# Where the weights of a feed-forward block lie between the forward and the backward pass of a decode step

## The chip, the core and the metric

The kernel runs on one core of a Trainium2 chip. The metric is device time in microseconds (us) of one execution, lower is better. The engines are TensorE (PE; its weight loads are PEld), VectorE (DVE), ScalarE (ACT), GpSimd (POOL) and SyncE (SP). Each works through its own queue in order. In this kernel SP issues the loads, POOL issues the stores, and 16 DMA engines carry both.

## What is computed

One token passes through a transformer block, and then the gradients of the block are formed. All tensors are bfloat16. Cut to what matters:

```python
h = layernorm(x) * (1 + ca) + sa            # sa, ca, ga, sb, cb, gb = silu(c) @ w_mod
q = (h @ wq)                                # 32 heads of 192
p = softmax(q @ k_cache.T * 192 ** -0.5)    # per head, 8192 keys
x1 = x + ga * ((p @ v_cache) @ wo)
h = layernorm(x1) * (1 + cb) + sb           # = xb
x2 = xb + hs(xb); x2 = x2 + gelu(layernorm(x2) @ w3) @ w4
out = x1 + gb * x2                          # D = 640, w3 640x1536, w4 1536x640
# and the gradients of x, k_cache, v_cache, wq, wo, w3, w4, c, w_mod for a given grad_out
```

(With a single token the shifted part `hs` is zero.) The outputs are `out` and the nine gradients. The K and V caches are 32 x 8192 x 192 each, 101 MB each, and their gradients are as large, so nearly all bytes are those four tensors.

## The kernel before, in words

**Tiles.** A head's K or V is handled in two half tiles of 128 partitions x 32 x 192 (1,536 KB, 1.57 MB). K has five buffers (`KB`, 0 to 4), V three (`VB`, 0 to 2). A further tile of this size has the tag `prod`: products of the scores in the forward pass, `pq` in the backward pass, and `w4a` in between. `w4b` (128 x 3840) holds pieces of w4, and `stg` of the same size is the staging tile of the backward. The backward pass also has `do_r`, `v_bc`, `dao_bc`, `wT` and two `er_b` tiles.

**Forward (lines 503 to 592).** A loop runs over heads 0 to 30. SP loads the next K and V halves as buffers come free (L344, L298), DVE and PE form the scores, ACT and DVE scale V by the softmax weights, PE accumulates K^T V for the later dq.

**Middle (L596 to L769, then L859 to L908).** Head 31 is done by itself: `score_mul` (L602) multiplies the K halves into `pb`, `score_tree` (L606) sums them on PE, `o_rows` (L407) forms the output. `pair_o` and `pair_ao` give x1. Then come two layernorms folded into one chain of small reductions (L709 to L741), u = w3^T n2 as 60 matmuls (L745), the gelu and its derivative on DVE and one exponential on ACT (L751 to L769), the product of du with the transposed w3 (60 matmuls, L875), a chain to `dao_bf` (L897), the products of wo with it (`do_mm`, L832), and the 60 matmuls of h2 = w4^T g (L857, `h2_mm`).

Where the weights lie in the middle:
- w3 rows 0 to 511 in `VB[0]` and the rest in a `vs` tile (L648, L650); w4 rows as `w4b` (blocks 0 to 3) and `w4a` (4 to 11, one load, L659); blocks 0 to 2 are loaded a second time into `stg` (L859).
- The transposed w3 goes to `VB[1]` (nine blocks) and `w4b` (three). `w3t` makes it in twelve groups of five PE transposes and one ACT copy (L667, L668), with a PSUM tile of two buffers. Five groups stand before the u matmuls, seven or eight behind.
- `dg_part` (L500) forms one entry of w4 dbo per block on DVE; twelve calls are strewn over the end of the forward pass and the middle.

**Backward (from L910).** 64 steps s go through the half heads, from head 31 down. In each step PE forms dV as outer products (`dv_groups`, L951; copied by ACT, L952), DVE forms V times do (`mul_q`, L931) and PE sums it (`tree_q`, L940) to dP, then DVE forms dK (`dk_part`, L956), and POOL stores both (L1193). The first five output tiles lie in `OB = (VB[1], KY, KE, VB[1], KD)`, where `KY`, `KE`, `KD` are K buffers. The first V tiles needed are those of head 31, still in `KY` and `VB[2]`; the third is loaded again into `VB[0]` (L918).

`late_rows` (L914) runs in the first step: dw4 is made row block by row block on DVE (L847), nine blocks in `VB[0]` and three in `stg`, and stored by POOL (L850). Other outputs and weights are side jobs: a list (L1135 on) from which `slot()` takes about one piece per call, four calls in each step. The order on each queue is the order of the code; the regions marked `manual_schedule` keep it, and small independent DVE operations may be moved between dependent ones.

Of the kernel before, what the change touches and what calls it, by code (L numbers as in the profile page):

```python
# [8 lines left out]
FP32 = mybir.dt.float32  # L9
# [11 lines left out]
def kernel(  # L21
# [27 lines left out]
    P = 128  # L49
# [277 lines left out]
    OB = (VB[1], KY, KE, VB[1], KD)  # L327
# [11 lines left out]
    with tc.tile_pool(name="vs", bufs=3) as vsp, tc.tile_pool(name="ft", bufs=2) as ft, \  # L339
            tc.tile_pool(name="psM", bufs=2, space=PS) as psM, tc.tile_pool(name="psO", bufs=2, space=PS) as psO, \  # L340
            tc.tile_pool(name="psR", bufs=2, space=PS) as psR:
        def load_k(h, t):
            kb = KB[(2 * h + t) % NKB]
            nc.sync.dma_start(out=kb, in_=K_hd[h][:, t * JH : (t + 1) * JH, :])  # L344
            return kb
# [147 lines left out]
        def w4r(a):  # L493
            if a < 3:
                return w4b[:, a * D : (a + 1) * D]
            return w4b[:, 5 * D : 6 * D] if a == 3 else w4a[:, a - 4, :]
# [6 lines left out]
        with tc.manual_schedule(engines=ORDER):  # L503
# [144 lines left out]
            nc.sync.dma_start(out=flat(VB[0])[:, 0 : 4 * F].rearrange("p (i n) -> p i n", i=4), in_=w3d[:, 0:4, :])  # L648
            w3_4 = vsp.tile([P, JQ, VW], BF16, name="vs").rearrange("p j d -> p (j d)")[:, 0:F]
            nc.sync.dma_start(out=w3_4, in_=w3d[:, 4, :])  # L650
# [7 lines left out]
            w4a = pp.tile([P, 8, D], BF16, name="w4a", tag="prod")  # L658
            nc.sync.dma_start(out=w4a, in_=w4v[:, 4:12, :])  # L659
            w3v = [flat(VB[0])[:, k * F : (k + 1) * F] for k in range(4)] + [w3_4]  # L660
            w3Tv = [flat(VB[1])[:, a * D : (a + 1) * D] for a in range(9)] + [w4b[:, a * D : (a + 1) * D] for a in range(3)]

            def w3t_gen():
                for a in range(NF):
                    tp = psr([P, 1024], BF16, "w3T_ps")
                    for k in range(ND):
                        T_.transpose(out=tp[:, k * P : (k + 1) * P], in_=w3v[k][:, a * P : (a + 1) * P], identity=ident_bf)  # L667
                    A_.copy(out=w3Tv[a], in_=tp[:, 0:D])  # L668
                    yield

            w3t_it = w3t_gen()

            def w3t(n):
                for _ in range(n):
                    next(w3t_it, None)

# [15 lines left out]
            pair_sum(po_x, 0, os_.pop(H1 - 1))  # L692
            pair_sum(po_x, 1, os_.pop(H1))
            er_t = [e_rows(TL, psB, "b")]
            w3t(1)
            o2 = pair_o(TL, po_x)
            ps_ao = pair_ao(o2, wo_l[TL], psB, "b")
# [5 lines left out]
            w3t(1)  # L703
# [6 lines left out]
            dg_part(1)  # L710
            w3t(1)
            m = mean_sum(ps, 1, "ln_m")
            xc = col(ND, "ln_xc1")
            V_.tensor_scalar(out=xc, in0=x1, scalar1=m[:, 0:1], scalar2=None, op0=ALU.subtract)
            pr = tcol(2 * ND, "ln_pr")
            V_.tensor_tensor(out=pr[:, 0:ND], in0=xc, in1=xc, op=ALU.mult)
            V_.tensor_tensor(out=pr[:, ND : 2 * ND], in0=xc, in1=a1, op=ALU.mult)
            ps = mean_mm(pr, 2 * ND)
            dg_part(1)
            w3t(1)  # L720
            vt = col(2, "ln_vt")
            V_.reduce_sum(out=vt, in_=ps[:, 0 : 2 * ND].rearrange("p (a b) -> p a b", b=ND), axis=AX.X)
            zz = col(ND, "ln_z")
            V_.tensor_scalar(out=zz, in0=pr[:, ND : 2 * ND], scalar1=vt[:, 1:2], scalar2=None, op0=ALU.subtract)
            pr = tcol(2 * ND, "ln_pr")
            V_.tensor_tensor(out=pr[:, 0:ND], in0=zz, in1=zz, op=ALU.mult)
            V_.tensor_tensor(out=pr[:, ND : 2 * ND], in0=zz, in1=sS2, op=ALU.mult)
            ps = mean_mm(pr, 2 * ND)
            r1, r2 = col(1, "ln1_r"), col(1, "ln2_r")
            rsq(vt[:, 0:1], r1)  # L730
            dg_part(1)
            xc2 = col(ND, "ln_xc2")
            V_.scalar_tensor_tensor(out=xc2, in0=zz, scalar=r1[:, 0:1], in1=sS, op0=ALU.mult, op1=ALU.add)
            w3t(1)
            ab = mean_sum(ps, 2, "ln_ab")
            v2 = col(1, "ln_v2")
            V_.tensor_scalar(out=v2, in0=ab[:, 0:1], scalar1=r1[:, 0:1], scalar2=ab[:, 1:2], op0=ALU.mult, op1=ALU.add)
            V_.tensor_scalar(out=v2, in0=v2, scalar1=r1[:, 0:1], scalar2=C_S[:, 0:1], op0=ALU.mult, op1=ALU.add)
            rsq(v2, r2)
            n2_bf = col(ND, "n2_bf", BF16)  # L740
            V_.tensor_scalar(out=n2_bf, in0=xc2, scalar1=r2[:, 0:1], scalar2=None, op0=ALU.mult)  # L741
            ups = psS.tile([P, NF], FP32, name="u_ps", tag="s")
            for a in range(NF):
                for k in range(ND):
                    T_.matmul(ups[:, a : a + 1], lhsT=w3v[k][:, a * P : (a + 1) * P], rhs=n2_bf[:, k : k + 1], start=(k == 0), stop=(k == ND - 1))  # L745
            dg_part(3)
            w3t(NF)
            u2, w_, t_, pd = (col(NF, n) for n in ("u2", "w_", "t_", "pd"))
            s_, g_, du = (col(NF, n) for n in ("s_", "g_", "du"))
            u = col(NF, "u")  # L750
            V_.tensor_copy(out=u, in_=ups)  # L751
            V_.tensor_tensor(out=u2, in0=u, in1=u, op=ALU.mult)
            V_.tensor_scalar(out=w_, in0=u2, scalar1=GELU_K1, scalar2=1.0, op0=ALU.mult, op1=ALU.add)
            V_.tensor_tensor(out=w_, in0=w_, in1=u, op=ALU.mult)
            A_.activation(out=w_, in_=w_, func=ACT.Exp, scale=-2.0 * GELU_K0)
            dg_part(NF)
            V_.tensor_scalar(out=u2, in0=u2, scalar1=3.0 * GELU_K1, scalar2=1.0, op0=ALU.mult, op1=ALU.add)
            V_.scalar_tensor_tensor(out=pd, in0=u, scalar=2.0 * GELU_K0, in1=u2, op0=ALU.mult, op1=ALU.mult)
            V_.tensor_tensor(out=pd, in0=pd, in1=d_g, op=ALU.mult)
            V_.tensor_scalar(out=w_, in0=w_, scalar1=1.0, scalar2=None, op0=ALU.add)  # L760
            V_.reciprocal(out=s_, in_=w_)
            V_.scalar_tensor_tensor(out=t_, in0=s_, scalar=-1.0, in1=pd, op0=ALU.add, op1=ALU.mult)
            V_.tensor_tensor(out=t_, in0=d_g, in1=t_, op=ALU.subtract)
            du_bf = col(NF, "du_bf", BF16)
            V_.tensor_tensor(out=du_bf, in0=t_, in1=s_, op=ALU.mult)
            V_.tensor_tensor(out=g_, in0=s_, in1=u, op=ALU.mult)
            V_.tensor_tensor(out=du, in0=t_, in1=s_, op=ALU.mult)
            g_bf = col(NF, "g_bf", BF16)
            V_.tensor_copy(out=g_bf, in_=g_)  # L769


# [10 lines left out]
    bst = ctx.enter_context(tc.tile_pool(name="bst", bufs=1))  # L782
    psV = ctx.enter_context(tc.tile_pool(name="psV", bufs=2, space=PS))
    psR = ctx.enter_context(tc.tile_pool(name="psR2", bufs=1, space=PS))
    psT = ctx.enter_context(tc.tile_pool(name="psT", bufs=1, space=PS))
    ctx.enter_context(tc.manual_schedule(engines=ORDER))
    R8 = JH // 4
    NS = 2 * HQ

    def load_er(s):  # L790

        er = bst.tile([P, R8, P], BF16, name="er_b", bufs=2)
        h, t = ht(s)
        r0 = (h % 2) * J + t * JH
        nc.gpsimd.dma_start(out=er[0:P:32, :, :], in_=er_t[0][r0 : r0 + JH, :])  # L795
        return er
# [5 lines left out]
    NDR = 6  # L802
    do_r = bst.tile([P, NDR, PW], BF16, name="do_r")

# [3 lines left out]
    stg0 = bst.tile([P, ND * CW], BF16, name="stg")  # L808
# [33 lines left out]
    def w4c(a):  # L842
        return stg0[:, (3 + a) * D : (4 + a) * D] if a < 3 else w4r(a)

# [7 lines left out]
    h2_ps = psV.tile([P, 2, 512], FP32, name="h2_ps", tag="v")[:, 0, 0:ND]  # L852

    def h2_mm(lo, hi):
        for k in range(lo, hi):
            for a in range(NF):
                T_.matmul(h2_ps[:, k : k + 1], lhsT=w4c(a)[:, k * P : (k + 1) * P], rhs=g_bf[:, a : a + 1], start=(a == 0), stop=(a == NF - 1))  # L857

    nc.sync.dma_start(out=stg0[:, 3 * D : 6 * D].rearrange("p (a r) -> p a r", a=3), in_=w4v[:, 0:3, :])  # L859
# [9 lines left out]
    V_.tensor_tensor(out=Gn, in0=G, in1=n2, op=ALU.mult)  # L869
    V_.scalar_tensor_tensor(out=Bv, in0=adb, scalar=r1[:, 0:1], in1=dy_c, op0=ALU.mult, op1=ALU.add)  # L870
    do_t(TL, 0)
    dn_ps = psR.tile([P, JH, TS], FP32, name="dot_ps")[:, 0, 0:ND]
    for k in range(ND):
        for a in range(NF):
            T_.matmul(dn_ps[:, k : k + 1], lhsT=w3Tv[a][:, k * P : (k + 1) * P], rhs=du_bf[:, a : a + 1], start=(a == 0), stop=(a == NF - 1))  # L875
# [228 lines left out]
    def g_dw3(lo, n):  # L1104
# [5 lines left out]
        if lo + n == ND:  # L1110
            next_w()
# [205 lines left out]
```

## Time and profile before

| | |
|---|---|
| time, median of 7 runs | 1436.74 us (1434.38 to 1441.0) |
| the profiled execution, its time | 1436.74 us |
| its span (first to last instruction) | 1435.0 us |
| moved by DMA in the span | 571.96 MB, mean 399 GB/s |
| share of the span busy | PE 83%, PEld 54%, DVE 77%, ACT 61%, POOL 10% |
| granted TensorE clock, mean | 0.720 of full speed |
| chain that ended last, by engine | PE 44%, DVE 29%, DMA 11%, ACT 7% |

The profile is of one execution. Its page gives busy time for each engine, forty slices of the span with busy shares in tenths, the granted TensorE clock, the DMA engines' share and GB/s, the chain of waits that ended last, and groups of instructions with their mean time and what ended the idle time before them. Other views are the timeline of an engine, the transfers with their issue and landing, and sums over windows of the span. Times in the views are us from the start of the span. The end of the forward pass lies near 540, the first store of the backward pass at 583.25.

### The profile page before, as it was taken

Reading aid. Unit: us, or ns where it says so; the run is one execution under the profiler, and the core shown is the slowest. Engines: PE = TensorE matmul, PEld = TensorE weight load, DVE = VectorE, ACT = ScalarE, POOL = GpSimd, SP = SyncE. Lnnn points to the kernel's source line nnn. Section 1 sums busy time; section 2 is a strip of 40 time slices with the busy share of each in tenths; the row PEclk is TensorE's granted clock in tenths of the full one; section 3 lists DMA queues with packets and bytes.
Section 4 is the critical chain, followed back from the end, with each engine's and each line's share of the span. In section 5 each row is a group of like instructions: output and inputs, shape, how many; then the busy total and the mean of one; then the engine's idle time right before and its main releaser. Section 6 shows DMA issues by size and latency. Waiting matters only on the chain.

```text
span 1435.0 us, 29991 instructions
## 1 busy us (share of the span) xinstructions
PE 1196.7 (83%) x12577; PEld 780.8 (54%) x12577; DVE 1109.3 (77%) x1395; ACT 880.5 (61%) x1923; POOL 138.4 (10%) x240
## 2 busy tenths in 40 slices
PE   3999999999999997787888787788888878688883
PEld 1677776777777676444444444444444444344541
DVE  4999999999999996666776776677677667567683
ACT  0777777777777773545565666566565666455653
POOL 0000000000000000111111111111111111111111
PEclk9999999999999996655555556555555556555555
DMA  9999999999999994699999999999999999999998
GB/s 374 398 418 419 415 417 394 414 421 413 417 414 414 420 413 181 259 393 424 418 403 421 425 414 413 421 416 425 412 418 415 420 417 414 367 380 412 387 361 366
DMA packets 77748, 571.96 MB, mean 399 GB/s; under 512 B 8590, under 2 KB 26718, under 8 KB 37294
## 3 DMA queue, kind: packets, MB, share of 16 engines
q1 hardware_dynamic: 51402, 343.59, 59.0%
q0 software_dynamic: 26192, 226.47, 38.3%
q8 instruction: 98, 1.61, 0.4%
q14 instruction: 36, 0.29, 0.1%
q10 hardware_dynamic: 20, 0.00, 0.0%
HBM read 343.58 MB, written 225.91 MB: 397 GB/s over the span
## 4 chain that ended last, share of the span: by engine, by line
PE 44%; DVE 29%; DMA 11%; ACT 7%; issue 7%; POOL 1%; SPq 0%; ACTq 0%; POOLq 0%; DVEq 0%
PE dot_ps L940 20%; DVE prod L303 8%; DMA KB<-in_A_k_cache_dram 7%; PE dv_ps L951 7%; DVE pq L931 6%; PE wT_ps L818 5%; DVE prod L308 4%; PE mp L384 4%; PE dot_ps L314 3%; DVE vs L362 3%; ACT wT L819 2%; PE mp L389 2%; ACT KB L952 2%; DMA out_dram<-KB 2%; DMA out_dram<-stg 1%
## 5 line engine op out<-in xcount | busy, mean ns | idle before, releaser
L952 ACT CAST KB<-dv_ps 128x768 bf16<-128x768 f32 x504 | 382.6, 804 | 270.8 <-PE dv_ps L951 270.1
L940 PE MATMUL dot_ps<-pq,ident_bf 128*128 128x256 bf16 x1536 | 359.5, 403 | 60.4 <-DVE pq L931 60.1
L369 ACT ACTIVATE vs<-VB,Ef 128x192 bf16<-128x192 bf16 x840 | 303.1, 442 | 0.0
L940 PEld LDWEIGHTS <-ident_bf 128*128 128x128 bf16 x1536 | 188.3, 133 | 186.1 <-issue 124.4
L951 PE MATMUL dv_ps<-do_r,er_b 1*128 1x192 bf16 x2048 | 222.0, 335 | 56.0 <-ACT KB L952 52.5
L956 DVE TENSOR_TENSOR KB<-qs_bc,dS 128x3072 bf16<-128x3072 bf16 x126 | 220.5, 1751 | 13.5 <-DMA out_dram<-KB 10.3
L303 DVE TENSOR_TENSOR prod<-KB,qs_bc 128x6144 bf16<-128x6144 bf16 x62 | 207.8, 3352 | 18.0 <-DMA KB<-in_A_k_cache_dram 10.3
L931 DVE TENSOR_TENSOR pq<-VB,do_r 128x3072 bf16<-128x3072 bf16 x126 | 220.5, 1750 | 0.0
L951 PEld LDWEIGHTS <-er_b 1*128 1x128 bf16 x2048 | 92.6, 111 | 176.1 <-issue 170.9
L384 PE MATMUL mp<-vs,KB 128*128 128x193 bf16 x1920 | 185.0, 249 | 0.0
L384 PEld LDWEIGHTS <-KB 128*128 128x128 bf16 x1920 | 165.3, 98 | 18.8 <-issue 6.3
L318 DVE TENSOR_REDUCE dP<-dot_ps 128x32 f32<-128x512 f32 x64 | 44.2, 691 | 147.5 <-PE dot_ps L940 147.5
L795 POOL DMA_DIRECT2D er_b<-er_t x64 | 41.0, 641 | 1152.7 <-PE w3T_ps L667 567.2
L314 PE MATMUL dot_ps<-prod,ident_bf 128*128 128x512 bf16 x372 | 97.2, 400 | 44.7 <-DVE prod L308 44.7
L362 DVE TENSOR_TENSOR vs<-VB,E 128x1728 bf16<-128x1728 bf16 x120 | 123.5, 1050 | 0.0
L308 DVE TENSOR_TENSOR prod<-prod 128x3072 bf16<-128x3072 bf16 x62 | 108.7, 1753 | 1.0
L819 ACT COPY wT<-wT_ps 128x1024 bf16<-128x1024 bf16 x84 | 80.8, 962 | 45.1 <-PE wT_ps L818 43.8
L389 PE MATMUL mp<-vs,KB 128*64 128x193 bf16 x1920 | 103.2, 250 | 0.0
L389 PEld LDWEIGHTS <-KB 128*64 128x64 bf16 x1920 | 77.2, 110 | 19.5 <-issue 19.5
L314 PEld LDWEIGHTS <-ident_bf 128*128 128x128 bf16 x372 | 37.7, 107 | 83.6 <-issue 56.3
L349 ACT ACTIVATE E<-S_h,negm 128x256 bf16<-128x256 f32 x30 | 15.2, 508 | 109.6 <-DVE negm L526 109.6
L1193 POOL DMA_DIRECT2D out_dram<-KB x127 | 68.5, 543 | 42.9 <-ACT KB L952 14.8
(333 smaller groups left out, 1017.5 us busy)
## 6 DMA issues: line engine op xcount, KB each, us to landing
VB<-in_A_v_cache_dram SPq DMA_DIRECT2D x125, 1536.0 KB, 11.7
out_dram<-KB POOLq DMA_DIRECT2D x125, 1536.0 KB, 14.3
KB<-in_A_k_cache_dram SPq DMA_DIRECT2D x64, 1536.0 KB, 11.8
wo_st<-in_A_wo_dram SPq DMA_DIRECT2D x30, 480.0 KB, 11.7
w_st<-in_A_wq_dram SPq DMA_DIRECT2D x12, 960.0 KB, 11.7
out_dram<-wo_st POOLq DMA_DIRECT2D x16, 480.0 KB, 18.4
out_dram<-w_st POOLq DMA_DIRECT2D x7, 960.0 KB, 18.1
w_st<-in_w_mod_dram SPq DMA_DIRECT2D x6, 960.0 KB, 18.1
```

The costliest lines, as they stand in the source:

```text
L303: V_.tensor_tensor(out=prod, in0=src, in1=vec[:, None, :].to_broadcast([P, JH, DH]), op=ALU.mult)
L308: V_.tensor_tensor(out=prod[:, :, 0:w], in0=prod[:, :, 0:w], in1=prod[:, :, w : 2 * w], op=ALU.add)
L314: T_.matmul(ps, lhsT=ident_bf, rhs=prod[:, :, k : k + TS], start=(k == 0), stop=(k == w - TS))
L362: V_.tensor_tensor(out=vs[:, 0:n, 0:DH].rearrange("p j (a b) -> p j a b", b=4), in0=v[:, v0 : v0 + n, :].rearrange("p j (a b) -> p j a b", ...
L369: A_.activation(out=vs[:, k, 0:DH], in_=v[:, v0 + k, :], func=ACT.Copy, scale=Ef[:, j0 + k : j0 + k + 1])
L384: T_.matmul(mp[:, 0:MW], lhsT=kb[:, j0 + k, 0:P], rhs=vs[:, k, 0:MW], start=(q == 0 and k == 0), stop=(z and k == JQ - 1), skip_group_chec ...
L389: T_.matmul(mp[p0 : p0 + 64, MO : MO + MW], lhsT=kb[:, j0 + k, P:DH], rhs=vs[:, k, 0:MW], start=False, stop=(z and k >= JQ - 2), skip_grou ...
L931: V_.tensor_tensor(out=pq[:, q], in0=v_l[s][:, q * JQ : (q + 1) * JQ, :], in1=do_of(ht(s)[0])[:, None, :].to_broadcast([P, JQ, DH]), op=AL ...
L940: T_.matmul(ps[:, q * JQ : (q + 1) * JQ, :], lhsT=ident_bf, rhs=pq[:, q, :, k : k + TS], start=(k == 0), stop=(k == DH - TS), skip_group_c ...
L951: T_.matmul(ps[:, b, k * DH : (k + 1) * DH], lhsT=er[p0 : p0 + 1, 2 * m + k, :], rhs=doh[p0 : p0 + 1, :], start=True, stop=True)
L952: A_.copy(out=dV4[:, 2 * q : 2 * q + 2, m * PW : (m + 1) * PW], in_=ps[:, :, 0:PW])
L956: V_.tensor_tensor(out=dK[:, lo:hi, :].rearrange("p j (a b) -> p j a b", b=4), in0=qh.rearrange("p (a b) -> p a b", b=4)[:, None, :, :].to ...
```

## The change

All of it lies in the middle and the first backward steps.

1. **w3** goes to the `prod` tile (rows 0 to 511, as `w3p`) and to the first 1536 columns of `w4b` (the rest). **w4** blocks 4 to 11 go to `VB[0]` in two loads (4 to 7 ahead of w3, 8 to 11 behind it). The second load of blocks 0 to 2 goes to `w4b`.
2. **VB[1]** is left alone: it still holds the V half of head 30 that step 2 needs, so that load falls away. The first output tiles become `(VB[0], KY, KE, VB[0], KD)`, and the order of V buffers follows.
3. **The transposed w3** goes, as 60 blocks of 128 columns, to tiles of the backward that are not in use yet: `do_r`, `stg`, `v_bc`, `dao_bc` and a new `w3x`. These tiles and the two `er_b` are made once, by name, ahead of the middle's second half. It is made eight blocks at a time (7 groups and a half): PE transposes and the copies are placed apart, one copy is on DVE. The PSUM pools of the backward are opened before the layernorm chain.
4. The transposes of E (`e_rows`) move behind the mean matmul of x1; some `dg_part` calls move.
5. The du matmuls go block by block ahead of the wo transposes (`do_t`). h2 is formed in two parts by blocks of w4 (3 to 11 ahead of `do_mm`, 0 to 2 behind it), in a PSUM tile that shares its buffer with the wo transposes.
6. **dw4** is made in `stg`: six blocks at the start, six later as a side job of two pieces; both are stored from there.
7. The second K half tile of head 31 is loaded in two transfers.

```diff
-    OB = (VB[1], KY, KE, VB[1], KD)
+    OB = (VB[0], KY, KE, VB[0], KD)
...
-            nc.sync.dma_start(out=kb, in_=K_hd[h][:, t * JH : (t + 1) * JH, :])
+            cut = (0, JQ, JH) if (h, t) == (H1, 1) else (0, JH)
+            for lo, hi in zip(cut[:-1], cut[1:]):
+                nc.sync.dma_start(out=kb[:, lo:hi, :], in_=K_hd[h][:, t * JH + lo : t * JH + hi, :])
...
-            nc.sync.dma_start(out=flat(VB[0])[:, 0 : 4 * F].rearrange("p (i n) -> p i n", i=4), in_=w3d[:, 0:4, :])
-            w3_4 = vsp.tile([P, JQ, VW], BF16, name="vs").rearrange("p j d -> p (j d)")[:, 0:F]
-            nc.sync.dma_start(out=w3_4, in_=w3d[:, 4, :])
+            nc.sync.dma_start(out=w4b[:, 0:F], in_=w3d[:, 4, :])
+            load_w4(4, 8)
             score_mul(1, 0)
...
-            w4a = pp.tile([P, 8, D], BF16, name="w4a", tag="prod")
-            nc.sync.dma_start(out=w4a, in_=w4v[:, 4:12, :])
+            w3p = flat(pp.tile([P, JH, DH], BF16, name="w3p", tag="prod"))
+            nc.sync.dma_start(out=w3p[:, 0 : 4 * F].rearrange("p (i n) -> p i n", i=4), in_=w3d[:, 0:4, :])
+            load_w4(8, NF)
...
+    w3at = [(buf, c) for buf, n in ((do_f, NDR * PW), (stg0, ND * CW), (v_bc, PW), (dao_bc, D), (w3x, 4 * P)) for c in range(0, n, P)]
+    def w3t_gen():
+        for n in range(0, NF * ND, 8):
+            if n % 16 == 0:
+                tp = psV.tile([P, 2, 1024], BF16, name="w3T_ps", tag="v")
...
+                T_.transpose(out=tp[:, n // 8 % 2, b * P : (b + 1) * P], in_=w3v[k][:, a * P : (a + 1) * P], identity=ident_bf)
...
-            dg_part(3)
-            w3t(NF)
+    w3t_out(A_.copy)
+    w3t_pe(2)
+    w3t_out(A_.copy)
+    dg_part(2)
...
     A_.activation(out=w_, in_=w_, func=ACT.Exp, scale=-2.0 * GELU_K0)
+    w3t_out(A_.copy)
+    w3t_pe(2)
...
+    w3t_out(A_.copy)
+    w3t_out(V_.tensor_copy)
...
+    nc.sync.dma_start(out=w4b[:, 0 : 3 * D].rearrange("p (a r) -> p a r", a=3), in_=w4v[:, 0:3, :])
...
-    do_t(TL, 0)
-    dn_ps = psR.tile([P, JH, TS], FP32, name="dot_ps")[:, 0, 0:ND]
-    for k in range(ND):
-        for a in range(NF):
-            T_.matmul(dn_ps[:, k : k + 1], lhsT=w3Tv[a][:, k * P : (k + 1) * P], rhs=du_bf[:, a : a + 1], start=(a == 0), stop=(a == NF - 1))
+    for a in range(NF):
+        for k in range(ND):
+            T_.matmul(dn_ps[:, k : k + 1], lhsT=w3Tb(a * ND + k), rhs=du_bf[:, a : a + 1], start=(a == 0 and k == 0), stop=(a == NF - 1), skip_group_check=True)
+    do_t(TL, 0)
...
-    h2_mm(0, 1)
+    h2_ps = psT.tile([P, 512], FP32, name="h2_ps", tag="t")[:, 0:ND]
+    h2_mm(range(3, NF))
...
-        dw4_rows(flat(VB[0])[:, 2 * D :], 5, 7)
-        dw4_store(flat(VB[0]), 3, 9)
-        v_l[2] = load_v(*ht(2), VB[0])
-        dw4_rows(stg0, 0, 3)
-        dw4_store(stg0, 0, 3)
+        dw4_rows(stg0[:, 2 * D :], 2, 4)
+        dw4_store(stg0, 0, 6)
...
+    def g_dw4():
+        dw4_rows(stg0, 6, 3)
+        yield
+        dw4_rows(stg0[:, 3 * D :], 9, 3)
+        dw4_store(stg0, 6, 6)
         yield
...
-    jobs = [(3, g_do(1)), (1 + ND // 4 + 1, g_bcast(dao, ND, dao_bc)), (1, g_dwo(0)), (4, g_bcast(du, NF, du_bc)), (1, g_dw3(0, 2)), (1, g_dwo(1))]
+    jobs = [(3, g_do(1)), (1 + ND // 4 + 1, g_bcast(dao, ND, dao_bc)), (1, g_dwo(0)), (2, g_dw4()), (4, g_bcast(du, NF, du_bc)), (1, g_dw3(0, 2)), (1, g_dwo(1))]
...
-        return (KY, VB[2], VB[0], VB[2])[s] if s < 4 else VB[(0, 2, 1)[(s - 4) % NVB]]
+        return (KY, VB[2], VB[1], VB[2], VB[1], VB[2], VB[0])[s] if s < 7 else VB[(1, 2, 0)[(s - 7) % NVB]]
 
-    v_l = {s: v_buf(s) for s in range(2)}
+    v_l = {s: v_buf(s) for s in range(3)}
```

## The prediction

> **What bounds the kernel now.** I read the page's slices first, then windows of the middle and of what follows, then the chain of waits there, then the transfers' issue times.
>
> ```profile
> PEclk9999999999999996655555556555555556555555
> DMA  9999999999999994699999999999999999999998
> ```
>
> The DMA engines are full in every slice but those at 538 to 610 us. There the loads of the forward pass have ended and the backward pass has nothing to store yet. The second view is windows (length, busy of PE, PEld, DVE, ACT, POOL, clock, DMA share, GB/s):
>
> ```profile
> 553.00:584.00 31.00, 22.62 (x300) 17.73 (x299) 23.22 (x95) 14.20 (x26) 2.13 (x4) 0.50 0.08 26
> 584.00:596.00 12.00, 11.32 (x96) 6.92 (x95) 8.00 (x12) 6.94 (x10) 3.93 (x6) 0.50 0.97 326
> 596.00:607.00 11.00, 8.38 (x111) 5.57 (x109) 4.38 (x4) 7.47 (x15) 1.08 (x2) 0.97 0.99 392
> 607.00:608.00 1.00, 0.04 (x1) 0.06 (x1) 0.79 (x3) 0.88 (x2) 0.71 (x2) 1.00 0.58 240
> ...
> 608.00:1228.00 620.00, 510.03 (x3792) 290.89 (x3792) 425.12 (x584) 366.56 (x529) 98.77 (x168) 0.55 1.01 416
> ```
>
> Three things carry the prediction. The hole is 31 us at a share of 0.08. From 608 to 1228 the engines are never free (1.01, 416 GB/s). And between the two the queue runs dry once, at 607 (0.58): all that was issued before has then been moved. The next traffic is a dV store:
>
> ```profile
> 595.25 0.53 POOL L1193 DMA_DIRECT2D out_dram<-KB  x1 [2.78 <-DVE KB L956]
> 604.68 0.64 POOL L795 DMA_DIRECT2D er_b<-er_t  x1 [8.90 <-PE dv_ps L951]
> 606.56 0.54 POOL L1193 DMA_DIRECT2D out_dram<-KB  x1 [1.24 <-ACT KB L952]
> ```
>
> It is issued when ACT has copied the last group of dV(1), so PE and ACT set when the full stretch begins. That stretch ends at 1228, where DVE had stood for a store to land:
>
> ```profile
> 1228.45 1.76 DVE L956 TENSOR_TENSOR KB<-qs_bc,dS 128x3072 bf16<-128x3072 bf16 x1 [8.07 <-DMA out_dram<-KB]
> ```
>
> So up to 1228 compute is 8 us ahead of the transfers. After it compute leads (window shares of 0.81 at 1240 to 1255 and 0.82 at 1360 to 1375), and the last transfers drain until 1431. Between 608 and 1228 bytes count; before 607 only the date of the dV(1) store counts.
>
> **The middle, step by step.** The chain of waits in the hole:
>
> ```profile
> 544.95 10.86 DMA w4a<-in_B_w_dram
> 555.83 0.83 DVE w4b L500
> ...
> 561.54 1.76 PE u_ps L745 x60
> ...
> 568.31 0.70 ACT w4b L668
> ...
> 570.25 1.74 PE dot_ps L875 x60
> ```
>
> *Scores.* DVE stood 1.66 us until the second K tile landed at 539.85. With the load in two halves the first (0.79 MB at 418 GB/s, 1.9 us less) is there at 538.0, DVE is free at 538.31: 1.6 us sooner. The V half issued at 536.72 lands 10.6 later, at 547.3, and is read at 548.28 now, so 0.9 remains. Loads queue without a gap here (share 1.00), so I cost the extra issue at SP's 0.33 us, beside other transfers. Bounds: 0 to -1.6.
>
> The Trainium skill (DMA: Bandwidth & Descriptors, Anatomy of one DMA, and Rules for kernel authors) speaks against halves: at least 1 MiB per transfer, about 2.0 us fixed for each. No row here isolates a fixed part. By the rule the second half would land up to 2 us later and the 0.9 would be lost; the middle's sum would be -1.3.
>
> *To x1.* The order listing of the changed program puts product sums of two w4 rows (0.82 + 0.08 each) before and inside the o chain. They use up the 0.9 and the 0.4 us that the transposes ahead of the wo matmuls cost now. The mean matmul of x1 ends at 554.2, as now.
>
> *To n2.* The 2.29 us stall on the whole w4 load goes: the row needed next lies in the part loaded first. What is late next is w3. Its 1.57 MB now go ahead of the last 0.66 MB, which at 360 GB/s take 1.8 us, so w3 lands at about 554.0. The mean is read at 554.4 instead of 556.58. PE has 8 transposes between reductions where it had 5 (0.71, so 1.15). n2 comes at 559.6 (561.25), the 60 u matmuls end at 561.95 (563.30). Were w3 the last to land (555.8), all this would be 1.2 later.
>
> *To du.* Today eight groups of transposes (0.70) and copies (0.69) in lockstep stand ahead of the exponential on ACT, at 568.89. In the changed order one group (1.15) and its copy (1.0) do: 564.1. DVE is next: two product sums, three small operations, then 1.05 us of chain as now, so du at 566.2 (570.02 + 0.17). The rest of the transposes (PE to 566.0, ACT to 566.6) end before the du matmuls reach their tiles.
>
> *To the first V product.* The wo transposes now lie behind the du matmuls: 1.01 us more ahead of the sums (570.15 for 572.91). h2's PSUM tile shares one buffer with them, so 45 h2 matmuls (0.029 each, 1.3) wait for the second wT copy (0.91) and stand ahead of the do matmul: 573.35 for 574.83. Behind it 15 h2 matmuls replace 48 (1.26). Also pq no longer waits for the last reader of w4a at 577.07. So dv starts at 574.85 (577.00) and the V product at 574.9 (577.17). **Middle: -2.2 us**, between -1.0 and -3.4.
>
> **Behind the middle.** PE at half clock sets the pace from 577 to 601, so six dw4 rows fewer (0.31 each) in DVE's start give nothing. The dV(1) store moves with the middle: 604.3.
>
> *The V tile kept.* The V loads on SP's queue go from 126 to 125, 1.57 MB less, 3.8 us at 416 GB/s. But that load ran between 591 and 601, before the queue ran dry. The changed kernel issues 5.7 MB until 597 (two dV halves, six dw4 rows, two dK halves, one V tile) where there were 8.3; from 582.5, at the 359 GB/s of the mean from 584.4 to 607.4, they end near 599. From there to 605 the engines would be idle. No DVE wait falls either: the V product at 601.98 followed its dS directly. I take **0**; it is -3.8 if the hole closes.
>
> *Six dw4 rows moved.* They are made on DVE in steps 1 and 2, and their store of 0.98 MB goes out near 613, in the full stretch: 0.98/416 = **+2.4 us**. Bounds: 0 if compute sets the end, 2.7 at 359 GB/s.
>
> *DVE there.* Three rows (0.98) and two dw3 rows (1.15) fall between products, the next two dw3 rows leave that place (-1.15), and the 3.5 us that DVE waits at 645 for a stg store should go, for the reader comes a half step later. The new stg store has some 14 us before its reader. Compute: -2.2 + 1.0 - 3.5 = -4.7, hidden while transfers lead. Nothing behind these on DVE's queue is a load; SP and POOL keep their order but for the moved store and the reload of three w4 rows, which lands (3.9 us) before it is read.
>
> Sum against the profiled run (1436.74 us, its span 1435.0, equal to the median of the seven): -2.2 + 0 + 2.4 = +0.2, so about **1436.8 us**.
>
> **Rivals.**
> - **A, bytes count throughout.** The early hole doesn't open, or what is gained there is kept: 1.57 MB less, dw4 only moved: -2.2 - 3.8 = -6.0, **1430.7**. For it: shares of 0.97 to 1.0 from 584 on. Against: the dry second at 607.
> - **B, compute sets the end.** PE, DVE and ACT lead the chain from 645 to 1206, and only some 12 us of DMA waits stand in it. Then -4.7: **1432.0**. Against: the 8.07 us at 1228.
> - **C, slower: the fast stretch of PE is lost.** The granted clock is 1.00 from 596.7 to 610.7 and 0.50 around it. Six matmuls of L940 take 0.83 there and 1.46 elsewhere, 32 of L1175 0.84 and 1.47, four of L951 0.34 and 0.50. Up to the dV(1) store that is 4 x 0.63 + 0.63 + 6 x 0.16 + 0.8 (two do products, 0.57 for 0.98) = 4.9, of which ACT's copies (0.80) hide some; I take 4. If the stretch comes later than the tree of step 1, the store and the full stretch come 4 us later: **1440.8**.
> - That the tile is loaded all the same is excluded by the count of loads.
>
> The Trainium skill (TensorE: Matmul & The Clock Gate, Part 1) says about 3.4 us of sustained matmuls bring the full clock. The trace differs: from 587 to 596 PE is busy 8.32 of 9.00 us at 0.50. By the rule C would be worth nothing.
>
> **How the numbers follow.** Forecast 0.37, A 0.20, B 0.15, C 0.20, rest 0.08 (0.03 faster, 0.05 slower). What this kernel's measurement can tell from no change is about 0.2%, 2.9 us. Faster: A, B and 0.03 = 0.38. Slower: C and 0.05 = 0.25. Same: 0.37. The range takes in A and C with a little room: 1430.3 to 1441.0. The forecast's own range is 1434.5 to 1439.0.
>
> **What would show it.** Right: the V product at about 575, an idle share between 599 and 605, the full stretch from about 605, DVE still waiting for a store near 1228. A is right if there is no idle share before 605; B if no engine waits for a store near 1228 and the last store is issued 4 to 5 us sooner; C if the clock stays 0.50 until 604. A first V product at 577 or later makes the middle wrong.

## The result, and the profile after

| | runs | median us | lowest to highest | profiled execution, span |
|---|---|---|---|---|
| before | 70 | 1434.42 | 1425.79 to 1449.09 | 1436.74, 1435.0 |
| after | 28 | 1441.83 | 1432.19 to 1446.73 | 1442.01, 1439.9 |

The ratio is 1.0045 (95% interval 1.0032 to 1.0059): slower by about 6.5 us. That is the sign to which I gave 0.25, and the time lies 0.8 us above the range's upper end of 1441.0. The profiled executions differ by 5.3 us.

Windows of the changed kernel (start and end, length, busy time of PE, PEld, DVE, ACT, POOL, granted clock, DMA share, GB/s):

```profile
553.00:584.00 31.00, 25.82 (x329) 20.10 (x328) 22.20 (x88) 16.35 (x26) 3.47 (x5) 0.56 0.22 76
584.00:596.00 12.00, 10.57 (x106) 7.01 (x105) 6.05 (x5) 7.00 (x11) 1.66 (x3) 0.70 0.85 290
597.00:602.00 5.00, 3.75 (x66) 2.55 (x67) 3.19 (x3) 3.58 (x9) 1.30 (x3) 1.00 0.05 19
608.00:955.00 347.00, 277.03 (x2104) 158.12 (x2100) 239.90 (x326) 202.16 (x294) 56.93 (x96) 0.57 1.01 417
955.00:1220.00 265.00, 216.83 (x1566) 123.34 (x1565) 176.75 (x252) 153.74 (x220) 40.42 (x68) 0.52 0.99 401
```

The first three lines are what the prediction described: the first stores come earlier, and then the engines stand idle from 597 to 602 (share 0.05). The full stretch begins some 5 us earlier than before, with this dV(1) store:

```profile
601.34 0.54 POOL L1229 DMA_DIRECT2D out_dram<-KB  x1 [1.25 <-ACT KB L982]
```

The surprise is the last line of the windows: 401 GB/s, where the kernel before moved 417 in the same window:

```profile
955.00:1220.00 265.00, 222.98 (x1638) 127.21 (x1636) 185.39 (x261) 160.75 (x230) 42.64 (x72) 0.55 1.01 417
```

Here the transfers no longer lead.

The start of each step shows where the lead went. A step is the time from one dP reduction on DVE to the next; the table gives the change in its start, after minus before:

| step | 0 | 4 | 16 | 28 | 32 | 36 | 40 | 44 | 48 | 49 | 63 |
|---|---|---|---|---|---|---|---|---|---|---|---|
| us | -5.1 | -6.4 | -3.8 | -4.4 | +1.7 | +2.1 | +2.1 | +7.0 | +8.4 | +5.1 | +4.8 |

The lead stands until step 28 (about 955 us). Steps 28 to 47 then take 273.5 us for 260.7, a loss of 12.8. The dP reductions that start steps 28 and 48, before the change and then after it:

```profile
956.20 0.69 DVE L318 TENSOR_REDUCE dP<-dot_ps 128x32 f32<-128x512 f32 x1 [2.65 <-PE dot_ps L940]
1216.85 0.69 DVE L318 TENSOR_REDUCE dP<-dot_ps 128x32 f32<-128x512 f32 x1 [1.91 <-PE dot_ps L940]
...
951.78 0.69 DVE L318 TENSOR_REDUCE dP<-dot_ps 128x32 f32<-128x512 f32 x1 [1.14 <-PE dot_ps L970]
1225.27 0.69 DVE L318 TENSOR_REDUCE dP<-dot_ps 128x32 f32<-128x512 f32 x1 [3.02 <-PE dot_ps L970]
```

In both runs those steps hold the same products, dV groups and stores of dK and dV.

What DVE waited for between 955 and 1220 (total us, times, longest) in the kernel before:

```profile
DVE dP L318 <- PE dot_ps L940: 54.8, 20, 5.9
DVE w_st L1042 <- ACT v_bc L1035: 10.9, 5, 3.1
DVE stg L1042 <- ACT v_bc L1035: 7.4, 4, 2.3
...
DVE dsc L1044 <- PE acc_ps L1040: 2.4, 1, 2.4
```

and in the changed kernel:

```profile
DVE dP L318 <- PE dot_ps L970: 53.0, 19, 6.5
DVE stg L1071 <- ACT v_bc L1064: 14.4, 4, 5.1
DVE w_st L1071 <- ACT v_bc L1064: 11.9, 4, 4.8
DVE dha L1073 <- PE acc_ps L1069: 4.8, 2, 2.4
DVE dsc L1073 <- PE acc_ps L1069: 2.4, 1, 2.4
```

The wait for dP is nearly the same. The waits of the weight chunks (`g_chunk`: on `v_bc` and `acc_ps`) are 20.7 us in the first and 33.5 in the second, 12.8 more: the size of the loss.

### The profile page after: what moved, and what is told of

Read it like the earlier page. It is cut to its first block, busy times and chain, and to the rows that moved or that the text cites. A ratio compares the mean times of both kernels' runs of the same rounds, so it can differ in the third digit from the quotient of the medians.

```text
span 1439.9 us, 29990 instructions
## 1 busy us (share of the span) xinstructions
PE 1185.3 (82%) x12577; PEld 776.2 (54%) x12577; DVE 1110.0 (77%) x1396; ACT 879.2 (61%) x1920; POOL 139.1 (10%) x240
## 4 chain that ended last, share of the span: by engine, by line
PE 39%; DVE 29%; DMA 12%; issue 9%; ACT 8%; POOL 1%; SPq 0%; ACTq 0%; POOLq 0%; DVEq 0%
PE dot_ps L970 18%; DVE prod L303 8%; DMA KB<-in_A_k_cache_dram 8%; PE dv_ps L981 7%; DVE pq L961 6%; PE wT_ps L857 4%; DVE prod L308 4%; DVE vs L364 3%; PE mp L386 3%; DMA out_dram<-KB 2%; PE dot_ps L314 2%; ACT wT L858 2%; ACT vs L371 2%; ACT KB L982 2%; DVE S_h L318 2%
## 5 line engine op out<-in xcount | busy, mean ns | idle before, releaser
L970 PE MATMUL dot_ps<-pq,ident_bf 128*128 128x256 bf16 x1536 | 355.3, 400 | 78.1 <-DVE pq L961 77.9
L314 PE MATMUL dot_ps<-prod,ident_bf 128*128 128x512 bf16 x372 | 94.0, 390 | 47.9 <-DVE prod L308 47.7
```

What stands on the lines that cost most here:

```text
L314: T_.matmul(ps, lhsT=ident_bf, rhs=prod[:, :, k : k + TS], start=(k == 0), stop=(k == w - TS))
L970: T_.matmul(ps[:, q * JQ : (q + 1) * JQ, :], lhsT=ident_bf, rhs=pq[:, q, :, k : k + TS], start=(k == 0), stop=(k == DH - TS), skip_group_c ...
```

## Two theories

A weight chunk is five pieces of the list of side jobs: 1 its vector; 2 first transposes; 3 the other transposes and `v_bc`; 4 the `acc_ps` matmuls and three rows scaled on DVE; 5 the sum with `acc_ps`, two more rows and a store. The list gives its pieces out evenly over 236 slots, four in each step: slot 0 behind dS, 1 behind the first V product, 2 behind the first half of dK, 3 at the end. `g_dw4` adds two pieces: 222 for 220.

**SLOTS**: all pieces behind `g_dw4` fall into later slots, and chunks whose pieces 3, 4, 5 fall into one step make DVE wait with the next V product queued behind. **BYTES**: what costs is the 0.98 MB of dw4 moved into the full stretch. **NEITHER**: the V tiles' new turn or the earlier start.

Step 35 shows what SLOTS means. In the changed kernel pieces 3, 4, 5 have slots 0, 1, 2, and the step takes 15.7 us. DVE there (start, length, idle time before it):

```profile
1047.98 1.75 DVE L961 TENSOR_TENSOR pq<-VB,do_r 128x3072 bf16<-128x3072 bf16 x1
1052.18 0.78 DVE L1071 TENSOR_SCALAR w_st<-v_bc,ha 128x384 bf16<-128x384 bf16 x3 [2.45 <-ACT v_bc L1064]
1052.88 1.75 DVE L986 TENSOR_TENSOR KB<-qs_bc,dS 128x3072 bf16<-128x3072 bf16 x1
1057.04 0.17 DVE L1073 TENSOR_TENSOR dha<-acc_ps,dha 128x5 f32<-128x5 f32 x1 [2.41 <-PE acc_ps L1069]
...
1057.57 1.75 DVE L961 TENSOR_TENSOR pq<-VB,do_r 128x3072 bf16<-128x3072 bf16 x1
...
1062.68 0.69 DVE L318 TENSOR_REDUCE dP<-dot_ps 128x32 f32<-128x512 f32 x1 [1.68 <-PE dot_ps L970]
```

DVE stands 2.45 us for `v_bc` and 2.41 for `acc_ps`. The second V product is ready to go all that time but queued behind them, and starts at 1057.57; PE then stands for it:

```profile
1059.38 0.37 PE L970 MATMUL dot_ps<-pq,ident_bf 128*128 128x256 bf16 x1 [1.62 <-DVE pq L961]
```

In the kernel before, the same step has pieces 4 and 5 in slots 0 and 1 and takes 13.2 us. Piece 3 lies in the step before it, so only 1.39 us are left to wait:

```profile
1049.88 0.85 DVE L1042 TENSOR_SCALAR w_st<-v_bc,ha 128x384 bf16<-128x384 bf16 x3 [1.39 <-ACT v_bc L1035]
1050.66 1.74 DVE L931 TENSOR_TENSOR pq<-VB,do_r 128x3072 bf16<-128x3072 bf16 x1
1052.32 0.15 DVE L1044 TENSOR_TENSOR dha<-acc_ps,dha 128x5 f32<-128x5 f32 x1
...
1054.52 1.74 DVE L931 TENSOR_TENSOR pq<-VB,do_r 128x3072 bf16<-128x3072 bf16 x1
```

Step 35 is not a clean pair, for the granted clock differs too: its mean there is 0.62 before the change and 0.50 after it. Step 31 is. It has pieces 4 and 5 in slots 0 and 1 before and 3, 4 and 5 in slots 0 to 2 after, DVE stands 1.64 us for `v_bc` before and 2.14 for `v_bc` and 2.42 for `acc_ps` after, and it takes 12.5 us and 15.4 at the same clock of 0.50 (before, then after):

```profile
993.89:1006.38 12.49, 10.96 (x84) 6.07 (x84) 9.09 (x14) 7.55 (x11) 1.75 (x3) 0.50 1.01 423
...
992.65:1008.03 15.38, 11.95 (x93) 7.10 (x93) 9.19 (x13) 8.62 (x13) 1.75 (x3) 0.50 1.02 408
```

Step 44 has pieces 3, 4 and 5 in both lists and takes 15.0 us in both, at 0.61 before and 0.50 after.

Placing both lists on the slots, steps 28 to 47 hold three steps with pieces 3, 4 and 5 before the change (13.9, 15.0, 15.3 us) and six after it (15.0 to 15.7).

## The experiments

All ratios are to the kernel before, run beside it on the same chip, with 95% intervals.

**e1, all of dw4 at the start.** From the changed kernel:

```
-        dw4_store(stg0, 0, 6)
+        dw4_store(stg0, 0, 6); dw4_rows(w4b, 6, 4); dw4_store(w4b, 6, 4)
+        dw4_rows(w4b[:, 5 * D :], 10, 1); dw4_store(w4b[:, 5 * D :], 10, 1)
+        dw4_rows(dao_bc, 11, 1); dw4_store(dao_bc, 11, 1)
-    ... (1, g_dwo(0)), (2, g_dw4()), (4, g_bcast(...
+    ... (1, g_dwo(0)), (4, g_bcast(...
```

> The changed kernel (1441.8 us median) with all twelve dw4 rows made and stored at the start: six in stg as now, five in the freed w4b, one in dao_bc; the two pieces of g_dw4 leave the list of side jobs (220 pieces as before). Theory BYTES (the 0.98 MB moved into the full stretch are what costs): 2.4 us less, about 1439.4. Theory SLOTS (two more pieces shift every later piece against the products of its step, and from step 28 on, where the profile of the changed kernel loses 13 us against before, compute is the chain): the whole loss goes, 1433 to 1436. Theory NEITHER (the loss comes from the V tiles' new turn or from the earlier start itself): within 1 us of 1441.8.

Measured: 1431.13 us, ratio 0.9966 (0.9942 to 0.9989). The whole loss goes and more (SLOTS gave 1433 to 1436), so NEITHER is out. The edit takes out pieces and moves bytes at once; the next two separate them.

**e2, two empty pieces in the kernel before.** A generator of two bare `yield`s in the list, where `g_dw4` stands in the changed one.

> The kernel before (1434.4 us median) with two empty pieces in the list of side jobs, behind g_dwo(0), where the change puts g_dw4: no instruction added, all later pieces stand up to two slots later. SLOTS: slower by 4 to 8 us, 1438 to 1442, lost between steps 28 and 48. BYTES and NEITHER: within 1 us of 1434.4.

Measured: 1445.34 us, ratio 1.0070 (1.0045 to 1.0095). Nothing was added but two empty turns, and the kernel loses 9.7 us, more than the 4 to 8 that SLOTS gave. From step 11 to 52 its profile runs beside the changed kernel's at a constant 4.1 to 4.2 us, steps 28 to 47 take the same 273.5 us, and the chunk waits between 955 and 1220 are the same 33.5. That the place of the pieces alone costs the time is shown; that it does so through DVE's waits is what e8, e9, e11 and e12 try.

**e3, the second half of dw4 left out.** The two pieces stay in the list, empty.

> The changed kernel whose two pieces of g_dw4 are empty: dw4 rows 6 to 11 are neither made nor stored (left out of the output), the list keeps its 222 pieces. BYTES: 2.4 us less, 1439.4. SLOTS: within 1.5 us of 1441.8, since the pieces stand where they did and DVE's 1.95 us lie early, where compute is ahead. If compute is the chain from the start of the full stretch on, up to 2 us less.

Measured: 1439.81 us, ratio 1.0024 (0.9997 to 1.0050). By the median the larger part of the loss stays, and the 2.0 us less are near the 2.4 of BYTES and above the 1.5 that SLOTS allowed. But the interval reaches from no loss at all to the whole of it. The profile is clearer: steps 28 to 47 take 273.4 us, as in the changed kernel.

**e4, the V tile loaded again.** In the changed kernel:

```
+        V_.memset(v_buf(2)[:, 0, 0:2], 0.0)
+        load_v(*ht(2), v_buf(2))
```

> The changed kernel with the kept V tile loaded again into its own place, 1.57 MB more, behind a tiny DVE write in the rows made at the start, so that the load runs between 585 and 597 as it did before. My forecast's term (the tile is worth 0, the engines have idle time until 602): within 1 us of 1441.8. Rival A of the prediction (bytes count throughout): 3.8 us more, 1445.6.

Measured: 1441.46 us, ratio 1.0043 (1.0018 to 1.0068), as the changed kernel. The load ran where the engines had room (share of 1.01 from 584 to 597, then 0.36 until 608). The tile is worth nothing that can be measured there: rival A's 3.8 us on top of the changed kernel's 1.0045 would be a ratio of 1.0071, just outside the interval. But in this list compute leads, so e10 repeats it in the other.

**e5, dw4's second half in pieces that exist.**

```
-    (1, g_dwo(0)), (2, g_dw4()), (4, g_bcast(du, NF, du_bc)),
+    (1, with_dw4(g_dwo(0))), (4, with_dw4(g_bcast(du, NF, du_bc))),
```

`with_dw4` runs one half of `g_dw4` in the first piece of the job that it wraps.

> The changed kernel with the two halves of g_dw4 put into pieces that the list has anyway (rows 6 to 8 in the piece of g_dwo(0), rows 9 to 11 and the store in the first piece of g_bcast(du)): same instructions, same store at nearly the same place, but 220 pieces. The first experiment took the 0.98 MB out of the full stretch and the two pieces out of the list at once; this one takes only the pieces out. SLOTS: as the first experiment, about 1431. BYTES: 2.4 us above it, 1433.5. If neither holds and the rows themselves cost, near 1441.8.

Measured: 1434.68 us, ratio 1.0002 (0.9978 to 1.0026). Taking the two pieces out of the count, and nothing else, gives 7.1 us back. Against e1 the late store costs 3.5 us, nearer to the 2.4 of BYTES than to nothing, with intervals that overlap a little. Its profiled execution was a long one, 1446.2, so its median counts here.

**e6, one empty piece.** As e2 with one `yield`.

> The kernel before with one empty piece in the list instead of two. SLOTS says that a step's length follows from the four pieces that fall into it: in the profiles so far a step with the pieces 3, 4, 5 of a weight chunk in its first three slots takes 15.0 to 15.7 us, one with 4, 5 in its first two 12.1 to 13.5, one with piece 5 first 11.6. By such a table of steps 8 to 58 this list costs 6 to 9 us more than the one of before, so 1440 to 1445 although it holds less than the list with two empty pieces. A cost that grows with the number of pieces would give half of the 9.7 us, 1440 or less.

Measured: 1431.20 us, ratio 0.9978 (0.9953 to 1.0002). My table of step lengths was wrong: this list is not slower. It is no cost per piece either, for one piece less than e2 makes 14 us. My table was read off two lists and didn't carry to a third; its profile has 68.5 us of chunk waits from 640 to 1400, the least of all unchanged chunks.

**e8, e9, the chunk's two waits removed** (in the changed kernel and in the one before):

```
-            ... in0=v_bc, scalar1=rows[:, i : i + 1] ...
+            ... in0=dao_bc[:, 0:PW], scalar1=rows[:, i : i + 1] ...
-        V_.tensor_tensor(out=acc, in0=ps, in1=acc, op=ALU.add)
+        V_.tensor_tensor(out=acc, in0=x_c, in1=acc, op=ALU.add)
```

> The changed kernel in which the two DVE instructions of a weight chunk that wait have nothing to wait for: the outer-product rows are scaled from dao_bc instead of v_bc, and the sum adds x_c instead of acc_ps. So dwq, the w_mod gradient, the input gradient and the gradient of c come out different; every instruction stays. SLOTS with its mechanism (DVE, in order, stands before these two in a slot where PE and ACT have not made their operand yet, and the next V product is queued behind): the DVE waits of 39 us on v_bc and 14 on acc_ps after step 8 go, the loss of 13 us between steps 28 and 48 goes with them, and the transfers lead: 1425 to 1432, and not above the kernel before with the same edit. If the waits only mirror PE's own work, within 3 us of 1441.8.

> The kernel before with the same edit (the rows from dao_bc, the sum with x_c). SLOTS with its mechanism: 1428 to 1434, since the transfers lead there from 608 to 1228 already, so it gains less than the changed kernel does, and the two come within 5 us of each other with the changed one ahead. If the waits only mirror PE's work: within 3 us of 1434.4.

Measured: 1419.50 us, ratio 0.9902 (0.9870 to 0.9934), and 1426.87 us, ratio 0.9945 (0.9921 to 0.9969). With the same instructions and less to wait for, the changed kernel falls by 22 us and the one before by 8, and their order turns round. Both end below what I had expected, and the changed kernel ends 7.4 us ahead, where I had allowed 5. So without these waits the loss is gone.

**e10, e13, on top of e1: the V tile loaded again as in e4, and a late first product.** In e13 `mul_q(0, 1)` is made twice more ahead of the first `mul_q(0, 0)`.

> The kernel of the first experiment (changed kernel, all dw4 rows at the start, 220 pieces; 1431.1 us) with the kept V tile loaded again between 585 and 597. The fourth experiment made the same load in the list of 222 pieces, where compute sets the end, and found no difference; here DVE waits 21 us for stores, so transfers set the pace. My forecast's term (the load fits in before the queue runs dry): within 1 us of 1431.1. Rival A (bytes count throughout): 3.8 us more, 1434.9. If the load pushes the first stores back behind it, up to 3 us more.

> The kernel of the first experiment with the second V product of step 0 made twice more ahead of the first, so that the first V product and the first stores come 3.4 us later (two products of 1.68 us); nothing else changes. My forecast's reading (before the queue runs dry only the date of the dV(1) store counts, and the middle's gain is kept to the end): 2.5 to 3.4 us more, 1433.6 to 1434.5. If the early lead is used up later by waits for stores: within 1 us of 1431.1.

Measured: 1430.82 us, ratio 0.9982 (0.9958 to 1.0006), and 1430.67 us, ratio 0.9973 (0.9948 to 0.9998), both as e1 by the medians. But the intervals are wide: on top of e1's 0.9966, A's 3.8 us would give e10 a ratio of 0.9992 and 2.5 to 3.4 us would give e13 0.9983 to 0.9990, and both lie inside. So neither the tile's price in this list nor that of a later start is settled. The start was later as meant (from the first product to dP of step 0 it is 12.2 us for 8.8). e13 waits 15.1 us for stores from 640 to 1400 where e1 waits 23.0, which would fit a lead that is handed back in such waits; but e10, with the same median, waits 5.3, so single executions don't show it.

**e11, e12, the rows one piece later.** In e1 and in the changed kernel; nothing is left out:

```
-        for i in range(3): V_.tensor_scalar(out=stg[:, i, :], in0=v_bc, ...
         yield
-        V_.tensor_tensor(out=acc, in0=ps, in1=acc, op=ALU.add)
-        for i in range(3, ND): V_.tensor_scalar(out=stg[:, i, :], ...
+        for i in range(ND): V_.tensor_scalar(out=stg[:, i, :], in0=v_bc, ...
+        V_.tensor_tensor(out=acc, in0=ps, in1=acc, op=ALU.add)
```

> The kernel of the first experiment with all five rows of a weight chunk scaled in its last piece, and the sum with acc_ps behind them, where three rows stood in the piece before and the sum ahead of the other two. Nothing is left out. SLOTS with its mechanism (DVE stands 52 us for v_bc and 13 for acc_ps before 1220 and after): v_bc has one slot more (3 us) to arrive and most of the 52 us go; transfers lead, so 1424 to 1429. If it is PE's load of the pieces and not DVE's stand that counts: 1431 plus or minus 2.

> The changed kernel with the same edit of the weight chunk (222 pieces, dw4's second half in the list). SLOTS with its mechanism: the loss against the list of 220 pieces goes, 1426 to 1434, and it stands within 4 us of the kernel beside it that has this edit and all of dw4 at the start. If DVE's stand does not matter: 1441.8.

Measured: 1425.42 us, ratio 0.9924 (0.9895 to 0.9953), and 1421.40 us, ratio 0.9900 (0.9871 to 0.9929). The second is the changed kernel with its 222 pieces, and it beats both kernels: 20 us below the changed one, 13 below the one before. It was to be 1426 to 1434. Its DVE waits from 955 to 1220:

```profile
DVE KB L986 <- DMA out_dram<-KB: 13.0, 5, 4.7
DVE dha L1073 <- PE acc_ps L1069: 5.9, 2, 3.6
DVE dsc L1073 <- PE acc_ps L1069: 3.6, 1, 3.6
DVE stg L1072 <- ACT v_bc L1064: 2.4, 3, 1.2
...
DVE w_st L1072 <- ACT v_bc L1064: 1.4, 1, 1.4
```

`v_bc` costs 3.8 us where it cost 26.3, and DVE now waits for stores (13.0, where the changed kernel had none in this window): the transfers lead again.

All kernels, by the waits of DVE from 640 to 1400 in one execution each:

| kernel | pieces | chunk waits us | store waits us | median us |
|---|---|---|---|---|
| e2 | 222 | 90.3 | 4.2 | 1445.3 |
| changed | 222 | 90.8 | 10.7 | 1441.8 |
| e4 | 222 | 90.7 | 10.8 | 1441.5 |
| e3 | 222 | 91.4 | 7.2 | 1439.8 |
| e5 | 220 | 71.7 | 42.2 | 1434.7 |
| before | 220 | 75.8 | 13.8 | 1434.4 |
| e6 | 221 | 68.5 | 29.5 | 1431.2 |
| e1 | 220 | 74.1 | 23.0 | 1431.1 |
| e10 | 220 | 78.7 | 5.3 | 1430.8 |
| e13 | 220 | 74.2 | 15.1 | 1430.7 |
| e9 | 220 | 12.0 | 63.7 | 1426.9 |
| e11 | 220 | 18.6 | 58.4 | 1425.4 |
| e12 | 222 | 30.4 | 40.4 | 1421.4 |
| e8 | 222 | 23.6 | 40.6 | 1419.5 |

(e8 and e9 keep some chunk waits because a row is written over the weights that PE still transposes.) Three groups stand apart: about 90 us of chunk waits, about 70 to 80, and 30 or less. Within a group the column doesn't order the kernels. The store column holds what the profile puts down to a store; in front of dK it leaves up to 9.5 us more (e11) without a releaser.

## Why the prediction was wrong, point by point

- *The middle, -2.2 us.* Right. The first V product starts at 573.23 for 577.17; 1.96 of that the forward pass had already gained in this execution (last d_g product ahead of the middle at 536.27 for 538.23), so the middle gave 2.0. The two products:

```profile
577.17 1.76 DVE L931 TENSOR_TENSOR pq<-KB,do_r 128x3072 bf16<-128x3072 bf16 x1
...
573.23 1.76 DVE L961 TENSOR_TENSOR pq<-KB,do_r 128x3072 bf16<-128x3072 bf16 x1
```

  The first store is 3.2 earlier, counted in the same way. From that d_g product to the first V product it is 38.4 to 38.9 us in the four traces with the old middle and 35.1 to 37.0 in the ten with the new one. The K tile's second half came in time: DVE's two products of it ran without idle time between them (3.42 us from 536.27), so the 2 us by which I said it could be late did not show. The section that I cited gives them for transfers issued from GpSimd, and SP issues this load.
- *The V tile kept, 0.* Borne out in the list of 222 (e4). In the list of 220 (e10) the medians agree, but 3.8 us are not excluded. The idle time that I named opened, at 597 to 602 instead of 599 to 605.
- *Six dw4 rows moved, +2.4.* Of that size in e1 against e5 (3.5) and e3 (2.0); neither interval excludes 0.
- *"Compute: -2.2 + 1.0 - 3.5 = -4.7, hidden while transfers lead."* This step failed. The sum counts the rows that move into steps 1 and 2 and leaves out that `g_dw4` lengthens the list: "SP and POOL keep their order", I wrote, and did not ask where the 213 pieces behind it land on DVE's queue. They cost 12.8 us between steps 28 and 48. The cover was what I had read off one row, the 8.07 us that DVE stood for a store at 1228; 12.8 is more than it held, so compute set the end. After the change that store wait is gone (1.9 us of store waits after 1220). The -3.5 in the sum failed as well: DVE's wait at 645 went, but the next writer of `stg` waits 8.82 us, at 668.76, which the sum doesn't have. It is not what cost the time, for the lead at step 10 is 5.2 us and was 5.1 at step 0.
- *The sum.* e5 is the change without the two pieces, and its ratio of 1.0002 is what the other terms had added up to (+0.2 us). So the sum came out, but not all its terms are shown singly. The omitted term is worth 7 us there and 9.7 in e2.
- *"Before 607 only the date of the dV(1) store counts."* Not settled: in the list of 220 a start 3.4 us later gave the same median (e13), with an interval that leaves room for the 3.4.
- *Rival A* (1430.7) fails here, as the idle share shows. Whether the missing 1.57 MB count once the chunk waits are gone is open: e8 is 7.4 us ahead of e9, and no run separates the tile from the middle there. *Rival B*'s condition came true, compute set the end, but at a price that the shifted list set, so the time rose and did not fall. *Rival C* has the right sign and about the right time for the wrong reason: the clock was 1.00 from 597 to 602 and the dV(1) store came 5.2 us earlier. In the profiled execution of e4 the clock did stay at 0.50 there (584 to 608), and from dP of step 0 to that of step 2 it took 30.2 us for 25.8, 4.4 more and close to the 4 I gave C. The four executions profiled at 0.50 there (e4, e5, e11, e12) lie 2.7 to 11.5 us above their kernels' medians, the ten others from 7.4 below to 6.2 above, which speaks for such a cost to an execution. All four have the new middle. How often the unprofiled executions lose the stretch is not known, so C may have a part in the medians; it is not the cause of the loss, for e2 loses 9.7 us with the old middle and the full clock from 582 to 599.

The Trainium skill (Perfetto Trace Analysis, Identifying the Most-Contended Engine) says to find the most contended engine, by occupancy or, for the DMA engines, by the bandwidth they use, and to optimise that one first. By it the subject here is the DMA engines, at a share of 0.96 to 1.01 from 608 to 1400 in both kernels, while DVE is busy 177 of 265 us. The runs speak against it: e12 moves the same bytes as the changed kernel and is 20 us shorter, with 60 us less of chunk waits on DVE.

## What to carry to other kernels

A list of side jobs that is spread over slots is part of the schedule: an entry added anywhere moves every entry behind it, so count what the moved pieces will stand before, not only what the new one costs. Where an in-order engine must consume what two other engines are still making, give the product one slot more before the consumer; that was worth 20 us here on the list of 222 (e12) and some 6 on the list of 220 (e11 against e1), and the two lists then lie 4 us apart, where they lay 10.7 apart. A full transfer queue does not prove that compute is covered: the slack is what the consumers wait for stores, and it has to be larger than whatever the edit adds to the other side.

## What the hardware showed unexpectedly

- The full clock comes in portions. Read in windows of 1 us, its stretches after step 2 last 3.4, 6.8 or 13.7 us, and kernels with the same list get many of them at the same places (the changed kernel, e2 and e4 all in steps 12, 18, 20, 24, 27, 36 and 40). Two windows of the changed kernel, one such stretch and the time behind it:

```profile
1072.00:1079.00 7.00, 4.47 (x47) 2.57 (x46) 3.06 (x13) 5.84 (x9) 1.72 (x3) 0.96 1.00 428
1081.00:1123.00 42.00, 37.93 (x262) 20.89 (x262) 28.03 (x38) 25.17 (x36) 6.61 (x11) 0.50 0.99 399
```

  For 42 us PE was busy 90% of the time on average and the clock stayed at 0.50. The Trainium skill (TensorE: Matmul & The Clock Gate, What's actually happening) says that one busy window of about 3.4 us brings the full clock. The portions agree with the window's length; how busy a window has to be, the page doesn't say, and a mean of 0.90 was not enough here.
- Steps 28 to 47 hold 7 portions of 3.4 us before the change and 3 after it. Of the 12.8 us, 9.4 are lost in the nine steps in which the kernel before has part of such a portion (30, 34, 35 and 42 to 47); steps 31 and 44 show that the pieces count at one clock and that a slot pattern can take the same time at two. No run holds the clock fixed, so how much of the 12.8 us is this and how much the waits alone stays open; the edit that takes the waits away gives the time back either way.
- The same kernel varies by 23 us over 70 executions (1425.8 to 1449.1). One profile gives the order of the work and its waits; only medians of several runs tell such changes apart.
